# One-step block maxima and first tokens in one stretch, pieces of the second down projection behind five products, late gates kept in SBUF, a denser phase one: a spectral layer with a gated feed-forward on one core

## The chip, the core and the metric

The kernel runs on one core of a Trainium2 chip. The core has a matrix engine (TensorE, PE in the profile; PEld is its weight load), VectorE (DVE), ScalarE (ACT), GpSimd (POOL), and SyncE (SP), whose queue issues all but one of the DMAs. The engines run side by side and wait for each other through semaphores; each takes its own instructions in program order. The metric is the device time in microseconds of one execution. The changed kernel, too, is written for one core.

## What is computed

The input is a sequence of 8192 tokens of width 448. It is normalised; one branch passes it through a Fourier layer (a real FFT over the 8192 positions, a block-diagonal complex two-layer network with four blocks of 112, a soft threshold, the inverse FFT), the other through a gated feed-forward of inner width 1792. The output joins both.

```python
xn = _layernorm(x)                                   # over the 448 channels
Xf = rfft2(xn, axes=(1, 2))                          # 8192 positions
hr = zr @ w1[0] - zi @ w1[1] + b1[0]                 # per block of 112
hi = zi @ w1[0] + zr @ w1[1] + b1[1]
hr, hi = hr * (hr > 0), hi * (hi > 0)
or_ = hr @ w2[0] - hi @ w2[1] + b2[0]
oi_ = hi @ w2[0] + hr @ w2[1] + b2[1]
or_, oi_ = soft(or_, 0.01), soft(oi_, 0.01)          # sign(v) * max(|v| - lam, 0)
s = irfft2(or_ + 1j * oi_)
g = silu((gelu(xn @ w_gate) * (xn @ w_up)) @ w_down)
return x + s * g
```

## The kernel before, in words

**Precision.** All large products run in 16 bit: each operand is split into a high and a low half, scaled by powers of two taken from its largest magnitude, and three of the four partial products are added in PSUM. So a weight tile must first be loaded (`wst`, 704 KB each), its block's maximum found over the whole tile (`gu_block`, `largest`), then be scaled and split (`gu_split`) into its high and low halves in `wt`. `largest` works in two steps: a product with the identity turns the maxima of the 128 partitions into a row (`bf`), VectorE reduces it (`mxr`), and a second product spreads the result over the partitions again. Fourteen weight tiles `f` form eight blocks: tile 0, tile 1, then pairs.

**Tokens.** The 128 x 64 positions are worked in 16 chunks of four tiles of 128 tokens. The feed-forward's inner width goes in two passes: pass 0 takes weight tiles 0 to 7, pass 1 tiles 8 to 13. Chunks 0 and 1 of pass 0 use plain products (`plain`); all others use a 2x2 scheme with seven products instead of eight (`unit`, products 1, 5, 6, 2, 3, 7, 4 in that order, called a1, a5 ... in the code), each `unit` for two weight tiles. For it `gu_comb` prepares sums and differences of the weights (`cb`). Pass 0's down projection goes to DRAM (`prt`); pass 1 adds its own (`down2`, seven products again, in pieces by `prod2`), takes tanh, and writes the gate `q (1 + tanh q)` of every chunk but the last to DRAM (`gsp`).

**The Fourier branch** has three phases: phase one (`chunk1`: normalise, split, first stage, and the transposed tokens to DRAM for the feed-forward), phase two (`group`: second stage, the two layers, threshold) and phase three (`tiles3`: last stage, times the gate from `gsp`, plus `x`, out). They run beside the feed-forward, whose order on PE is fixed by the generator `ffn`.

**What sets the order.** A small planner in the kernel (`Pace`) runs all parts as Python generators on a clock of its own with assumed costs per instruction (`cost`), and emits each engine's instructions in the order in which it meets them; nothing is reordered on the chip. Constants give due times: `T1` and `DT` start phase one's chunks, `END2` and `END3` spread phases two and three, `yield ev(...)` waits in the plan for another part, `pe()` for PE. `Either` (`B`) puts an elementwise operation on VectorE or GpSimd, whichever ends first in the plan.

**Beginning.** `begin` loads the four tiles of chunk 0, computes mean and variance (`stats`: bn_stats, a power on GpSimd, four small steps on VectorE) for tiles 0 and 2, normalises them, then does the same for tiles 1 and 3; `token` splits and transposes each tile on PE into `xta`. Beside it `weights` finds and splits the weight blocks, and starts the maxima of the down weights once tile 1 is split.

**End.** A chunk of pass 1 stops before the last pieces of its `down2`; `state["tail"]` holds them, and the next chunk runs them after two of its first unit's products. The last chunk runs them itself. Each quarter of its gate then waits for phase three's last tiles in `s4`, and is multiplied, added to `x` and stored.

## Time and profile before

| | |
|---|---|
| median of 3 runs | 1820.6 us (1819.4 to 1821.87) |
| profiled execution | 1818.44 us, of which its span 1816.3 us |
| PE busy | 1768.8 us, 97% of the span |
| PE weight loads | 1422.6 us, 78% |
| VectorE busy | 1401.5 us, 77%, 2410 instructions |
| ScalarE busy | 1098.1 us, 60% |
| GpSimd busy | 588.0 us, 32%, 637 instructions |
| DMA | 287.78 MB, mean 158 GB/s; 289 to 328 GB/s in the slices from 1544 to 1771 us |

The profile is one execution. Times in it count from its first instruction; the execution's own time has 2.1 us more than its span. A row of the timeline gives start, duration, engine, source line, operation, tiles, and in brackets how long the engine stood idle before and what released it. All of the kernel's instructions bear one line (that of a recording helper), so they are told apart by their tiles. PE's durations overlap, since products are pipelined: the distance from one start to the next is what a product costs.

### The profile page before, as it was taken

The numbers are of one execution on the slowest core, as the hardware profiler recorded it, in microseconds if no ns is written. First come the engines' busy times: TensorE is split into PE (matmuls) and PEld (weight loads), VectorE is DVE, ScalarE is ACT, GpSimd is POOL, SyncE is SP. The second block draws the span as 40 slices with busy tenths as digits, with TensorE's granted clock in tenths as the row PEclk, the third lists the DMA queues.
The fourth block names the chain that finished last, engine by engine and source line by source line (L and its number), as shares of the span: only waits on it lengthen the run. The fifth ranks groups of instructions, "written<-read, shape, count | busy, mean of one in ns | idle before, by whom it ended". The sixth has DMA issues, their size and how long they took to land. (4 is left out here: it accounts for less than half of the span.)

```text
span 1816.3 us, 39111 instructions
## 1 busy us (share of the span) xinstructions
PE 1768.8 (97%) x15649; PEld 1422.6 (78%) x15649; DVE 1401.5 (77%) x2410; ACT 1098.1 (60%) x2105; POOL 588.0 (32%) x637
## 2 busy tenths in 40 slices
PE   6999999999999999999999999999999999999997
PEld 3446677767777677787887899999998998888886
DVE  7857778867777665666766888888878887878888
ACT  4736566645566555566767777777777765444443
POOL 3324443422443432000101223435343432433332
PEclk9999999999999999999999999999999999999999
DMA  6444665466666454113336634443434436999985
GB/s 254 154 124 152 172 193 157 149 195 185 180 183 194 134 152 126 38 55 100 78 103 174 157 93 119 118 105 87 115 91 118 114 89 171 321 293 328 289 295 184
DMA packets 345654, 287.78 MB, mean 158 GB/s; under 512 B 231840, under 2 KB 312736, under 8 KB 345472
## 3 DMA queue, kind: packets, MB, share of 16 engines
q1 hardware_dynamic: 345328, 285.26, 54.2%
q8 instruction: 122, 2.00, 0.5%
q14 instruction: 60, 0.49, 0.1%
q10 hardware_dynamic: 144, 0.03, 0.0%
HBM read 129.47 MB, written 106.61 MB: 130 GB/s over the span
## 5 line engine op out<-in xcount | busy, mean ns | idle before, releaser
L182 PEld LDWEIGHTS <-wt 128*128 128x128 f16 x9350 | 907.0, 98 | 181.8 <-issue 18.5
L182 PE MATMUL bk<-xta,wt 128*128 128x256 f16 (+1 forms) x5190 | 636.2, 276 | 11.7 <-ACT u L182 4.8
L182 PE MATMUL bk<-xtb,wt 128*128 128x256 f16 x3120 | 382.0, 273 | 1.7 <-ACT v L182 1.7
L182 PE MATMUL bk<-dw,h 128*128 128x448 f16 (+1 forms) x2208 | 373.4, 320 | 4.9 <-DVE h L182 3.3
L182 PEld LDWEIGHTS <-h 128*128 128x128 f16 x2688 | 258.4, 98 | 136.6 <-DVE h L182 4.9
L182 ACT COPY v<-bk 128x512 f32<-128x512 f32 x208 | 121.4, 584 | 89.8 <-PE bk L182 89.1
L182 ACT COPY u<-bk 128x512 f32<-128x512 f32 x208 | 121.5, 585 | 76.7 <-PE bk L182 73.4
L182 POOL TENSOR_TENSOR wt<-wt 128x256 f32<-128x256 f32 x100 | 78.5, 785 | 216.3 <-DVE wt L182 159.8
L182 DVE TENSOR_TENSOR u<-bk,u 128x512 f32<-128x512 f32 x104 | 71.5, 688 | 79.1 <-PE bk L182 73.7
L182 POOL TENSOR_TENSOR zs<-t,zs 112x256 f16<-112x256 f32 (+2 forms) x34 | 30.0, 884 | 262.0 <-ACT zs L182 258.7
L182 PE MATMUL bk<-dw,wt 128*128 128x224 f16 (+1 forms) x864 | 104.0, 269 | 4.8 <-DVE pt L182 4.8
L182 ACT ACTIVATE u<-u,fc 128x512 f32<-128x512 f32 (+1 forms) x118 | 77.7, 669 | 44.5 <-DVE u L182 44.1
L182 DVE SCALAR_TENSOR_TENSOR pt<-bk,fb,pt 128x448 f32<-128x448 f32 x112 | 75.2, 678 | 35.8 <-PE bk L182 35.0
L182 ACT ACTIVATE th<-bk,fb 128x448 f32<-128x448 f32 x64 | 40.4, 633 | 99.2 <-PE bk L182 63.6
L182 ACT CAST h<-wt 128x512 f16<-128x512 f32 (+1 forms) x128 | 68.6, 538 | 41.1 <-DVE wt L182 31.9
L182 DVE TENSOR_TENSOR v<-bk,v 128x512 f32<-128x512 f32 x104 | 71.2, 684 | 19.7 <-PE bk L182 19.1
L182 PE MATMUL bf<-w2t,wn 112*128 112x112 f16 x1512 | 84.9, 213 | 0.0
L182 PEld LDWEIGHTS <-wn 112*128 112x128 f16 x1512 | 80.7, 98 | 3.0
L182 POOL TENSOR_TENSOR v<-v,u 128x512 f32<-128x512 f32 x32 | 47.5, 1485 | 97.1 <-ACT v L182 96.9
L182 PEld LDWEIGHTS <-w1t 112*112 112x112 f16 x612 | 68.1, 130 | 7.6 <-issue 3.4
L182 ACT ACTIVATE th<-pt 128x448 f32<-128x448 f32 x64 | 36.8, 576 | 58.8 <-DVE pt L182 48.9
L182 DVE SCALAR_TENSOR_TENSOR gl<-v,fc,gl 128x512 f32<-128x512 f32 (+1 forms) x70 | 47.1, 690 | 32.4 <-ACT gl L182 31.0
(198 smaller groups left out, 2978.3 us busy)
## 6 DMA issues: line engine op xcount, KB each, us to landing
wst<-in_gu SPq DMA_DIRECT2D x22, 704.0 KB, 5.3
xts<-sx SPq DMA_DIRECT2D x32, 480.0 KB, 3.0
x<-in_x SPq DMA_DIRECT2D x17, 896.0 KB, 6.2
t<-ysb SPq DMA_DIRECT2D x64, 224.0 KB, 3.1
prt<-th SPq DMA_DIRECT2D x64, 224.0 KB, 2.0
pt<-prt SPq DMA_DIRECT2D x64, 224.0 KB, 3.9
u<-t SPq DMA_DIRECT2D x32, 448.0 KB, 5.9
y<-t SPq DMA_DIRECT2D x30, 448.0 KB, 3.5
```

Source lines behind the costliest of these rows:

```text
L182: return self.pace.issue(self.name, kind, out, ins, lambda: fn(out, *args, **kw))
```

## The change

- **Maxima.** For up to four columns `largest` sends each column, broadcast over 128 columns, through a product with the identity, which leaves the 128 partition maxima as a row on every partition, and one reduction on VectorE ends it. The floor moves into the operation before.
- **First tokens.** The statistics of all four tiles come first, on two small tiles of their own; then tiles 0 and 2 are normalised, then block 0's maximum runs with the second root between its product and its reduction, then tiles 1 and 3. The identity's cast moves from VectorE to ScalarE. The planner chooses the engine of the copies into `xta`. The first plain product pair takes high weights ahead of low ones.
- **Weights.** Blocks 1 to 4 are started after tile 0, the down weights' maxima after tile 4 instead of tile 1.
- **Phase one** begins at 78 instead of 84 on the planner's clock and takes 36 instead of 40 per chunk; `END2` and `END3` are 10 and 30 earlier.
- **Pass 1's down projection.** `down2` stops after three products' first pieces; the rest comes in five pieces, behind products a1, a5, a6, a2 and a3 of the next chunk's first unit. The last chunk has an order of its own (`down2_last`): four accumulations, and the two last quarters end behind the same last product.
- **Gates.** Chunks whose gates are not yet made when phase three is opened keep them in SBUF, in `s4`, which chunk 15 used alone before: chunks 9 to 14. Their tiles of phase three run when the chunk's `down2` has begun, and `s4` is handed on by an event (`gfree`).
- **Planner's cost** of a 16-bit copy on VectorE, and more operations of the end left to `Either`.

```diff
-    def largest(dst, src, floor):
+    def largest(dst, src, floor, between=None):
...
+        if w <= 4:
+            for i in range(w):
+                T.matmul(b[:, 128 * i:128 * i + 128], src[:, i:i + 1].to_broadcast([128, 128]), identf,
+                         start=True, stop=True)
...
+            V.tensor_reduce(dst, b[:, 0:128 * w].rearrange("p (i k) -> p i k", i=w), axis=AXIS.X, op=ALU.max)
...
-    T1, DT = 84.0, 40.0
+    T1, DT = 78.0, 36.0
...
-            V.tensor_tensor(mx, fm[:, 0, :, b], fm[:, 1, :, b], op=ALU.max)
+            V.scalar_tensor_tensor(mx, fm[:, 0, :, b], 2.0 ** -30, fm[:, 1, :, b], op0=ALU.max, op1=ALU.max)
...
-        yield from largest(mxa, mx, 2.0 ** -30)
+        yield from largest(mxa, mx, 2.0 ** -30, None if b else (ev("reduced"), ev("root")))
...
     def down2(i, h, last):
+        done("pre", i)
         yield from last()
         x = yield from BD.get()
         yield from prod2(1, i, h, x, 0, 2, first=True)
-        z = yield from BY.get()
+        z = yield from BD.get()
         yield from prod2(2, i, h, z, 0, 2, first=True)
         y = yield from BD.get()
         yield from prod2(5, i, h, y, 0, 2, first=True)
-        yield from prod2(1, i, h, x, 2, 3)
-        e = pace.spawn(add2(i, QS[0], x), pace.last)
-        yield from prod2(2, i, h, z, 2, 3, last=True)
-        yield e
-        pace.spawn(ended2(i, QS[0], z, BY), pace.last)
-        yield from prod2(6, i, h, x, 0, 2)
...
+        def after_a1():
+            yield from prod2(1, i, h, x, 2, 3)
+            m[1] = pace.spawn(add2(i, QS[0], x), pace.last)
+            yield from prod2(2, i, h, z, 2, 3, last=True)
...
+        def after_a5():
+            yield m[1]
+            yield from prod2(6, i, h, x, 0, 2)
...
-        state["tail"] = tail
+        state["tail"] = [after_a1, after_a5, after_a6, after_a2, after_a3]
+
+    def down2_last(i, h, last):
...
     def ended2(i, qq, b, R):
...
+        if state.get("direct", NG) <= i < NG - 1:
+            if state["direct"] < i:
+                yield ev("gfree", i - 1)
+            V.scalar_tensor_tensor(blk(state["last"][0], *qq), th, 1.0, q, op0=ALU.add, op1=ALU.mult)
...
-    END1, END2, END3 = T1 + NG * DT + 12.0, 1460.0, 1780.0
+    END1, END2, END3 = T1 + NG * DT + 12.0, 1450.0, 1750.0
...
     def phase3():
...
+        def near():
+            for i in range(i0, NG):
+                if i < NG - 1:
+                    yield ev("pre", i)
+                for c in (2 * i, 2 * i + 1):
+                    pace.spawn(load3(c))
...
     def weights():
...
-        for b in range(PB[0][1]):
+        pace.spawn(gu_block(0, 0))
+        yield ev("w", 0)
+        for b in range(1, PB[0][1]):
             pace.spawn(gu_block(b, 0))
         combs = pace.spawn(gu_combs(near))
-        yield ev("w", 1)
+        yield ev("w", 4)
```

The order that the planner makes of it is seen at three places. First VectorE at the beginning, around block 0's maximum (`fm`, `fx`, `mxr`; `st` are the statistics, `x_102` is chunk 0's tokens), in the kernel before:

```order
L182 TENSOR_SCALAR x_102<-x_102,st 128x448
L182 TENSOR_REDUCE fm<-wst 128x2
L182 TENSOR_SCALAR x_102<-x_102,st 128x448
L182 COPY fx<-fm 128x2
L182 BN_STATS st<-x_102 128x6
L182 BN_AGGR st<-st 128x2
L182 BN_STATS st<-x_102 128x6
L182 BN_AGGR st<-st 128x2
L182 TENSOR_SCALAR st<-st 128x2
L182 TENSOR_REDUCE mxr<-bf 2x1
L182 TENSOR_TENSOR xs<-x_102,xs 128x448
L182 TENSOR_SCALAR fx<-bf 128x2
```

and in the changed kernel:

```order
L184 TENSOR_SCALAR x_102<-x_102,st 128x448 x2
L184 TENSOR_REDUCE fm<-wst 128x2
L184 TENSOR_SCALAR fx<-fm 128x2
L184 TENSOR_TENSOR st<-st 128x2 x2
L184 TENSOR_SCALAR st<-st 128x2
L184 TENSOR_TENSOR st<-st 128x2
L184 TENSOR_TENSOR xs<-x_102,xs 128x448
L184 TENSOR_REDUCE fx<-bf 128x2
```

Four statistics and one reduction no longer stand between the block's maximum and its factors; both normalisations of tiles 0 and 2 now stand ahead of the weight tile's reduction.

Second VectorE at a change of chunk in pass 1, one of the late ones. `pt` are the four quarters of the chunk that ends, each added to twice out of a PSUM bank; `u1` and `v1` belong to the first unit of the next chunk; `th` and `s4` take the gates. Before:

```order
L182 SCALAR_TENSOR_TENSOR pt_22156<-bk1_67,fb_79,pt_22156 128x448
L182 SCALAR_TENSOR_TENSOR pt_22257<-bk0_66,fb_79,pt_22257 128x448
L182 SCALAR_TENSOR_TENSOR pt_22156<-bk0_66,fb_79,pt_22156 128x448
L182 SCALAR_TENSOR_TENSOR pt_22257<-bk1_67,fb_79,pt_22257 128x448
L182 SCALAR_TENSOR_TENSOR g2_22546<-bf_22679,ms_92,g2_22546 128x448
L182 SCALAR_TENSOR_TENSOR th_22690<-th_22690,pt_22156 128x448
L182 SCALAR_TENSOR_TENSOR pt_22365<-bk0_66,fb_79,pt_22365 128x448
L182 TENSOR_TENSOR u1_22619<-bk3_69,u1_22619 128x512
```

and now:

```order
L184 SCALAR_TENSOR_TENSOR pt_22184<-bk1_67,fb_79,pt_22184 128x448
L184 SCALAR_TENSOR_TENSOR pt_22245<-bk0_66,fb_79,pt_22245 128x448
L184 SCALAR_TENSOR_TENSOR g2_22504<-bf_22673,ms_92,g2_22504 128x448
L184 TENSOR_TENSOR u1_22586<-bk2_68,u1_22586 128x512
L184 TENSOR_TENSOR x2_22502<-g2_22504,x2_22502 128x448
L184 SCALAR_TENSOR_TENSOR pt_22184<-bk0_66,fb_79,pt_22184 128x448
L184 SCALAR_TENSOR_TENSOR g2_22504<-bf_22716,ms_92,g2_22504 128x448
L184 TENSOR_TENSOR v1_22659<-bk4_70,v1_22659 128x512
L184 SCALAR_TENSOR_TENSOR pt_22245<-bk1_67,fb_79,pt_22245 128x448
L184 SCALAR_TENSOR_TENSOR s4_19980<-th_22740,pt_22184 128x2x224
```

The additions of the ending chunk, which stood in one run ahead of the next unit, are now spread among that unit's own additions.

Third VectorE at the very end, before:

```order
L182 SCALAR_TENSOR_TENSOR pt_23403<-bk1_67,fb_79,pt_23403 128x448
L182 TENSOR_TENSOR s4_20190<-pt_23315,s4_20190 128x2x224
L182 SCALAR_TENSOR_TENSOR th_23821<-th_23821,s4_20190 128x448
L182 TENSOR_TENSOR th_23821<-th_23821,x4l_20191 128x448
L182 TENSOR_TENSOR s4_20190<-pt_23403,s4_20190 128x2x224
L182 SCALAR_TENSOR_TENSOR th_23835<-th_23835,s4_20190 128x448
L182 TENSOR_TENSOR th_23835<-th_23835,x4l_20191 128x448
L182 SCALAR_TENSOR_TENSOR pt_23511<-bk0_66,fb_79,pt_23511 128x448
L182 TENSOR_TENSOR s4_20190<-pt_23511,s4_20190 128x2x224
L182 SCALAR_TENSOR_TENSOR th_23852<-th_23852,s4_20190 128x448
L182 TENSOR_TENSOR th_23852<-th_23852,x4l_20191 128x448
```

and now:

```order
L184 SCALAR_TENSOR_TENSOR pt_23341<-bk1_67,fb_79,pt_23341 128x448
L184 SCALAR_TENSOR_TENSOR pt_23414<-bk1_67,fb_79,pt_23414 128x448
L184 SCALAR_TENSOR_TENSOR th_23770<-th_23770,s4_19980 128x448
L184 TENSOR_TENSOR s4_19980<-pt_23341,s4_19980 128x2x224
L184 TENSOR_TENSOR th_23770<-th_23770,x4l_19981 128x448
L184 SCALAR_TENSOR_TENSOR th_23781<-th_23781,s4_19980 128x448
L184 TENSOR_TENSOR th_23781<-th_23781,x4l_19981 128x448
L184 TENSOR_TENSOR s4_19980<-pt_23414,s4_19980 128x2x224
L184 SCALAR_TENSOR_TENSOR th_23790<-th_23790,s4_19980 128x448
L184 TENSOR_TENSOR th_23790<-th_23790,x4l_19981 128x448
```

Two additions out of the last bank, and the rest of three quarters, now stand behind the last product; before it was one quarter's addition, and its three further steps.

228 lines of the change are left out of this document (175 added, 53 removed).

## The prediction

> **What bounds the kernel now.** I read the page first, then a table of windows, the waits by window, and the timeline of the two ends and of one change of chunk.
>
> ```profile
> PE 1768.8 (97%) x15649; PEld 1422.6 (78%) x15649; DVE 1401.5 (77%) x2410; ACT 1098.1 (60%) x2105; POOL 588.0 (32%) x637
> ```
>
> PE is busy 97% of the span, so only its idle time can be won, 47 us in all; the change takes away no product to speak of. The windows (busy time of PE, PEld, DVE, ACT, POOL, then granted clock, DMA share, GB/s) say where that idle time lies:
>
> ```profile
> 0.00:10.00 10.00, 0.75 (x4) 0.37 (x4) 4.14 (x12) 2.05 (x3) 2.04 (x7) 1.00 0.76 267
> 10.00:20.00 10.00, 4.37 (x22) 2.20 (x22) 9.52 (x26) 4.79 (x9) 3.23 (x3) 1.00 0.64 261
> 40.00:50.00 10.00, 8.48 (x51) 4.05 (x49) 10.00 (x20) 4.31 (x10) 4.62 (x5) 1.00 0.73 282
> 50.00:60.00 10.00, 8.28 (x47) 3.90 (x45) 8.97 (x25) 8.25 (x19) 3.59 (x3) 1.00 0.12 25
> 100.00:800.00 700.00, 692.88 (x5246) 508.14 (x5245) 498.06 (x899) 399.02 (x729) 230.98 (x287) 1.00 0.54 153
> 800.00:1500.00 700.00, 695.99 (x7322) 617.04 (x7320) 564.11 (x953) 503.15 (x1025) 209.74 (x198) 1.00 0.42 109
> 1500.00:1800.00 300.00, 292.07 (x2613) 252.30 (x2612) 247.18 (x364) 136.23 (x243) 111.08 (x105) 1.00 0.87 279
> 1800.00:1810.00 10.00, 6.45 (x61) 5.59 (x59) 7.65 (x12) 1.79 (x3) 1.14 (x1) 1.00 0.21 78
> 1810.00:1816.30 6.30, 0.00 (x0) 0.00 (x0) 3.14 (x6) 0.58 (x1) 0.00 (x0) 0.52 0.29 95
> ```
>
> In the first 20 us PE idles 14.9, from 40 to 60 us 3.2, from 100 to 800 us 7.1, from 800 to 1500 us 4.0, from 1500 to 1800 us 7.9, behind 1800 us 9.9. The opening has more idle time than it shows, since a product's duration covers the gaps to the next. The products of the first 57.2 us, by shape:
>
> ```profile
> L182 PE MATMUL bk<-xta,wt 128*128 128x512 f16 x72 | 17.6, 380 | 0.0
> L182 PE MATMUL bk<-xta,wt 128*128 128x256 f16 x44 | 7.6, 316 | 4.9 <-DVE wt L182 3.1 <-ACT wt L182 1.8
> L182 PE MATMUL bf<-xs,m 128*128 128x448 f16 x18 | 4.4, 353 | 0.0
> ```
>
> In a full run of such products (below) one of 256 columns comes every 0.11 us, so one of 512 costs about 0.215 and one of 448 0.19: 72, 44 and 18 of them are 15.5 + 4.8 + 3.4 us, and the 64 transposes, at under 0.11 each, and the maxima add some 6. So PE had about 30 us of work in 57 us. There the kernel is bound by the weights, which VectorE, ScalarE and GpSimd must make ready.
>
> **The opening, worked through the new order.** These rows of the timeline are what the old opening waits for:
>
> ```profile
> 8.95 1.22 DVE L182 TENSOR_REDUCE fm<-wst 128x2 f32<-128x1024 f32 x1 [1.47 <-DMA wst<-in_gu]
> 10.72 0.59 PE L182 MATMUL bf<-identf,fx 128*2 128x128 f32 x2 [1.84 <-DVE fx L182]
> 13.70 0.16 DVE L182 TENSOR_SCALAR fe<-fx 128x2 int32<-128x2 int32 x1
> 14.90 1.32 ACT L182 ACTIVATE wt<-wst,fc 128x512 f16<-128x512 f32 x2
> 17.74 2.25 DVE L182 SCALAR_TENSOR_TENSOR wt<-wst,fc,wt 128x512 f16<-128x512 f32 x2
> 23.47 1.80 PE L182 MATMUL bk<-xta,wt 128*128 128x256 f16 x8
> 23.58 0.62 DVE L182 COPY xta<-bk 128x896 f16<-128x896 f16 x1
> 27.70 1.70 PE L182 MATMUL bk<-xta,wt 128*128 128x256 f16 x14
> 30.55 2.32 PE L182 MATMUL bk<-xta,wt 128*128 128x256 f16 x11
> 31.05 0.66 DVE L182 TENSOR_TENSOR wt<-wst,wt 128x512 f16<-128x512 f32 x1
> 40.26 0.61 DVE L182 TENSOR_REDUCE dmx<-wo 128x1 f32<-128x448 f32 x1
> 41.38 0.98 DVE L182 TENSOR_TENSOR fx<-fm 128x2 f32<-128x2 f32 x1
> 52.64 0.16 DVE L182 TENSOR_SCALAR fe<-fx 128x2 int32<-128x2 int32 x1
> 55.74 1.16 POOL L182 TENSOR_TENSOR wt<-wst,wt 128x512 f16<-128x512 f32 x1 [3.04 <-ACT wt L182]
> 57.21 1.90 PE L182 MATMUL bk<-xta,wt 128*128 128x512 f16 x8
> ```
>
> Weight tile 0 lands at 8.95 whatever the order. Now two normalisations, about half a microsecond each, stand ahead of its reduction: it ends at 11.2 rather than 10.17. The pair of products with the identity is twice as long (the row at 10.72: 0.59 with its tail), to about 12.5; the second root and a split hide behind it, one reduction ends at 13.2, and three small steps at 13.8, where the old one was at 13.86. So block 0 gains nothing; behind it two copies of tokens stand ahead of ScalarE's split, which ends at 16.9 instead of 16.22. What is won stands later on VectorE: nothing is left between, so tile 0's low halves end at 18.4 instead of 19.99. The remaining tokens are in `xta` at 24.6, no sooner than the old 24.2. Block 1's product stands on PE behind the first 22 products and the transposes, to about 23; its factors follow at 24.2, ScalarE's four steps at 27.2, the last low half at 28.5, where the row at 31.05 ends at 31.71. Weight tile 1's products start at 28, where the old ones start at 30.55: **2.5 us** is the lower bound.
>
> The upper bound comes from tile 4. It waited for block 3's maximum, 11 us from `fx` at 41.38 to `fe` at 52.64, because two products and two reductions stood in queues among the down weights' reductions (eight like that at 40.26, 4.9 us on a VectorE that is busy 10.00 of 10). Now that is one product and one reduction, and the eight come after tile 4. From 28 on each tile is 22 x 0.215 plus a first-stage group of 0.57, 5.3 us, so tile 4 can start at 28 + 15.9 = 44 instead of 57.21; my count of the work of ScalarE and VectorE up to there ends at 43.4. What PE had done of chunk 1 by 57.2, 32 transposes and two first-stage groups, 3.5 us, is then still to do. That leaves **9.7 us**; with some waits left I take **8**. Bounds 2.5 and 11.
>
> **A rule on PE's clock.** Eight products take 1.80 us at 23.47 and fourteen 1.70 at 27.70: 0.21 and 0.11 us from start to start, though the windows show 1.00. The Trainium skill (TensorE: Matmul & The Clock Gate, Part 1: The HAM clock gate) says that the array runs at half clock until it has been busy for some 3.4 us, and falls back after as long an idle stretch. The durations agree with it, the granted clock in the table does not show it. By that rule the new opening, with a longer idle stretch ahead of its products, might run all of its first products slow.
>
> **Phase one, denser.** Same work on other due times. It is hidden as far as PE, busy 692.88 of 700, stays fed. The largest waits there:
>
> ```profile
> PE bk L182 <- ACT u L182: 4.8, 2, 3.4
> ```
>
> One of these, of 3.4 us, is a chance of due times; the new ones may lose it or make another. I take 0, bounds -4 and +4.
>
> **Pieces behind five products.** PE's waits from 800 to 1500 us (first row) and from 1500 to 1800 us:
>
> ```profile
> PE bk L182 <- DVE pt L182: 1.8, 6, 0.7
> PE bk L182 <- DVE h L182: 2.9, 5, 1.1
> PE bk L182 <- DVE pt L182: 2.2, 10, 0.3
> PE bk L182 <- ACT h L182: 0.6, 2, 0.3
> ```
>
> `pt` and `h` are those of the down projection: the additions that free a bank for the next piece, and the last unit's halves, needed by the pieces ahead of the next chunk. With six or more products between, 1.3 us each, both are covered. At most 1.8 + 2.9 + 2.2 + 0.6 = 7.5 us; the last chunk's share stays. I take **4.5**, bounds 0 and 7.5.
>
> **Gates in SBUF.** Six chunks drop their stores and loads of
>
> ```profile
> L182 SPq DMA_DIRECT2D gsp<-th x60: 539/551/1614, 1047.6 to 1771.7; - x60
> L182 SPq DMA_DIRECT2D g<-gsp x30: 326/434/1587, 1526.9 to 1785.5; - x30
> mt<-c_mt SPq DMA_DIRECT2D x32, 192.0 KB, 6.5
> ```
>
> 24 of 60 and 12 of 30 (the third row, from the page's list of issues, is a table that every tile of phase three loads: 6.5 us from issue to landing). The last 300 us have the DMA at 0.87, but PE's waits there name a DMA for 0.4 us in all, so this is worth nothing by itself. In return a late chunk's eight additions and products of phase three stand in one stretch of VectorE (busy 247 of 300), and 53 elementwise operations leave GpSimd for it. I take a loss of **1**, bounds -1 and +6.
>
> **The end.**
>
> ```profile
> 1803.67 1.31 PE L182 MATMUL bk<-dw,wt 128*128 128x224 f16 x12 [1.57 <-DVE pt L182]
> 1807.48 0.74 PE L182 MATMUL bk<-wt,h 128*128 128x224 f16 x6
> 1810.62 0.68 DVE L182 SCALAR_TENSOR_TENSOR pt<-bk,fb,pt 128x448 f32<-128x448 f32 x1
> 1812.71 0.63 DVE L182 TENSOR_TENSOR th<-th,x4l 128x448 f32<-128x448 f32 x1
> ```
>
> PE ends at 1808.2 and VectorE 5.1 later. The new order loses the wait of 1.57 and the smaller ones, 2 us at most. But two quarters now hang on the last product: ten VectorE operations of 0.62 to 0.68 stand behind it, 6.4 us instead of 5.1. I take a gain of **0.5**, bounds -1.5 (a loss) and 2.5.
>
> **Sum.** 1818.4 (the execution shown) - 8 - 4.5 + 1 - 0.5 = 1806.4. The median of the runs lies 2.2 above that execution: **1808.6**; I say 1808.
>
> **Rivals.**
> 1. *The weights stay late.* VectorE, at 9 to 10 of 10 between 30 and 60 us, still sets the pace, and only tile 1's 2.5 us arrive. For it: the maximum of block 0 is no sooner. Against it: five microseconds of reductions are gone from that stretch. 1808 + 5.5 = 1813.
> 2. *The pieces bring nothing*: they wait for the same VectorE, which has more to do. For it: `pt` now stands among the unit's additions. 1808 + 4.5 = 1812.
> 3. *Slower: one `s4` for six chunks.* A gate may only be written when the last chunk's tiles of phase three are added. If those come late, by their loads behind a full DMA, the writing instruction stands first on VectorE, and behind it the additions `u1` and `v1` on which PE's next products depend. Against it: a chunk has some 49 us for it (fifteen chunks' stores of `gsp` lie between 1047.6 and 1771.7). It decides from 12 : 6 = 2 us per chunk; with the table's landing of 6.5 us late in five of the six, half of it hidden, 16 us: 1824.
> 4. *All of it arrives*: 11 + 7.5 + 2.5 and no loss: 1820.6 - 21 = 1799.6, or 1797 with a phase one that loses its wait.
> 5. *A slow first stretch.* All of the first tile's 44 products come at 0.21 instead of 0.11: 4.4 us, of which the old opening, with 14 of them, paid 1.4. Up to 3 us of the 8 go: 1811. The Trainium skill (TensorE: Matmul & The Clock Gate, Part 1: The HAM clock gate) has a rule of this kind, told above.
>
> **How the numbers follow.** Forecast 0.50, rivals 0.14, 0.11, 0.08, 0.13, 0.04. Two medians of this kernel can be told apart from about 0.2%, 3.6 us. The forecast's own bounds reach from 1797 to just under 1820.6; the range 1797 to 1819 leaves out the slower rival and the far ends. Faster by over 0.2% means below 1817: all but the slower rival and the upper ends of the others, 0.83; the same 0.10; slower 0.07.
>
> **What would show it.** Right: `fm` near 10 us and one `fx` reduction near 13; weight tile 4's products near 44 to 47 us and PE full from there; no `dmx` reduction before that; PE's waits for `pt` and `h` behind 800 us under 3 us; PE's last product some 6 us ahead of VectorE's last. Wrong: VectorE or ScalarE holding weight tiles 2 to 4 past 50 us; waits of PE for `u` or `v` in the late chunks, behind an `s4` write on VectorE; or new waits between 100 and 800 us of the size of the gain.

## The result and the profile after

The changed kernel takes **1802.2 us** (median of 1799.7, 1802.21 and 1802.29) against 1821.2 us for the kernel before beside it: a ratio of **0.9891, interval 0.9878 to 0.9905**, or 19 us less. Executions that the record marks as slow are left out (6600.5 us of this kernel, 4794.9 us of the one with three `th` below, 2050.1 us of the one before); the second of them is the profiled one, so that kernel has no usable trace. The prediction said 1808, between 1797 and 1819. The total is inside the range. The parts that were to make it up are not what the prediction took them for, as the experiments show.

The page of the changed kernel, first part (busy time, share of the span, instructions):

```profile
span 1800.5 us, 38996 instructions
PE 1763.0 (98%) x15653; PEld 1427.5 (79%) x15653; DVE 1405.0 (78%) x2457; ACT 1100.5 (61%) x2103; POOL 541.4 (30%) x584
```

The work is the same (VectorE 1405.0 us for 1401.5), GpSimd has 47 us less, and the span is 15.8 us shorter. The profiled execution of before (1818.4 us) lies under all its other ones on record, so the traces show 16 of the 19 us. The windows, in the columns of the prediction:

```profile
10.00:20.00 10.00, 6.86 (x36) 4.51 (x37) 7.03 (x18) 4.61 (x10) 3.01 (x3) 1.00 0.74 286
40.00:50.00 10.00, 10.00 (x58) 5.17 (x57) 8.82 (x19) 9.68 (x20) 5.46 (x5) 1.00 0.94 313
50.00:60.00 10.00, 10.00 (x57) 4.93 (x56) 10.00 (x23) 7.58 (x16) 5.35 (x5) 1.00 0.75 256
100.00:800.00 700.00, 692.14 (x5346) 512.31 (x5345) 523.39 (x945) 411.11 (x761) 216.64 (x272) 1.00 0.55 156
800.00:1500.00 700.00, 695.88 (x7252) 617.84 (x7250) 554.30 (x954) 495.87 (x1002) 181.60 (x168) 1.00 0.42 106
1500.00:1785.00 285.00, 284.15 (x2561) 248.55 (x2560) 237.88 (x362) 131.74 (x231) 104.57 (x96) 1.00 0.86 257
```

PE is full from 30 to 60 us. In the two long stretches its idle time has hardly moved (7.9 us for 7.1, 4.1 for 4.0). From 1500 to 1785 us 0.85 us is left; before it was 7.0 in the same window (the prediction's 7.9 reach to 1800).

**Where PE stands.** The number of products is the same but for four, all of them products of the maxima, so the two kernels can be compared at equal work: for each I added up the columns of all products (those of the maxima left out) in order of their starts, and took the time at which the same sum is reached. This is the lead over the kernel before, in us; a minus is a lag. The other rows are the kernels of the experiments below.

| kernel | at 100 us | 500 | 1000 | 1500 | 1700 | 1780 |
|---|---|---|---|---|---|---|
| changed | 6.8 | 3.6 | 4.3 | 5.4 | 12.3 | 15.3 |
| changed, old opening | -0.7 | -2.8 | -2.0 | 2.8 | 4.9 | 7.8 |
| changed, down weights' maxima early | 5.3 | 1.2 | 1.8 | 2.0 | 6.3 | 8.1 |
| changed, old pieces | 6.3 | 4.7 | 5.4 | 0.3 | 3.0 | 3.1 |
| changed, gates through DRAM | 6.6 | 3.7 | 4.4 | 5.4 | 10.3 | 10.3 |
| changed, old phase one | 6.4 | 9.1 | 8.6 | 2.1 | 6.2 | 8.9 |
| before, new opening | 4.7 | 7.4 | 4.7 | 0.7 | -5.0 | -5.5 |
| before, pieces | 0.6 | -1.5 | -1.5 | -5.7 | -3.3 | -1.0 |
| before, dense phase one | -2.0 | -4.7 | -4.0 | -10.8 | -14.5 | -17.8 |
| before, pieces and dense phase one | -0.4 | -2.9 | -2.2 | 2.6 | 0.9 | 2.7 |

Each row is one execution, so small differences are no evidence. The new opening put alone into the kernel before, for one, was profiled in an execution of 1828.1 us, where its median is 1824.1, and the dense phase one alone in one of 1838.9, where it is 1835.0. A microsecond or so at 100 us can come from PE's rate: 6 to 25 of the first weight tile's 44 products came at half rate in these traces (0.21 us from start to start instead of 0.11), and with the same new opening 11 to 18.

The changed kernel wins 6.8 us in the opening, loses 3 of them in phase one by 500 us, wins 1.8 from there to 1500 us and 10 behind that.

**The opening.** Rows of the timeline of the changed kernel, in the order in which the prediction worked through them:

```profile
9.82 1.22 DVE L184 TENSOR_REDUCE fm<-wst 128x2 f32<-128x1024 f32 x1
...
11.39 1.20 PE L184 MATMUL bf<-identf,fx 128*128 128x128 f32 x4 [11.39 <-DVE st L184]
...
13.37 0.16 DVE L184 TENSOR_SCALAR fe<-fx 128x2 int32<-128x2 int32 x1
...
16.92 1.42 DVE L184 SCALAR_TENSOR_TENSOR wt<-wst,fc,wt 128x512 f16<-128x512 f32 x2 [2.55 <-ACT wt L184]
...
16.94 2.53 PE L184 MATMUL bk<-xta,wt 128*128 128x256 f16 x11 [1.75 <-ACT wt L184]
...
23.28 0.91 ACT L184 COPY xta<-bk 128x896 f16<-128x896 f16 x1 [0.42 <-PE bk L184]
...
24.18 0.19 ACT L184 ACTIVATE fc<-fh 128x1 f32<-128x1 f32 x1
...
28.21 0.59 PE L184 MATMUL bk<-xta,wt 128*128 128x512 f16 x2
...
44.93 0.82 PE L184 MATMUL bk<-xta,wt 128*128 128x512 f16 x3
```

Block 0's maximum is done at 13.5 us (worked out: 13.8), tile 0's low halves at 18.34 (18.4), the tokens at 24.2 (24.6), block 1's factors at 24.4 (24.2). Weight tile 1's first product starts at 28.21 (28), weight tile 4's, the 67th of 512 columns, at 44.93 (44). In the kernel before the 67th starts here:

```profile
55.50 0.82 PE L182 MATMUL bk<-xta,wt 128*128 128x512 f16 x3
```

The prediction's row at 57.21 was thus already inside tile 4. The eight reductions of the down weights follow where the prediction has them, four of them being

```profile
L184 DVE TENSOR_REDUCE dmx<-wo x4: 604/605/607, 52.8 to 60.2; 128x1 f32<-128x448 f32 x4
```

(instances; least, median and largest ns; first and last start), all behind 52 us, while PE no longer waits for them.

**The waits of PE**, from 800 to 1500 us (first row) and from 1500 to 1785 us (what is waited for; us in all, times, longest):

```profile
PE bf L184 <- DVE k L184: 4.1, 6, 1.1
PE bf L184 <- DMA mt<-c_mt: 0.5, 1, 0.5
PE bk L184 <- DVE h L184: 0.4, 1, 0.4
```

Not one wait for `pt` is left, and of 2.9 + 0.6 us for `h` 0.4; the 1.7 us for `v` behind 1500 us that the kernel before had, too, are gone. In their place phase two costs more (`k`: 4.1 us for 2.0).

**The end.**

```profile
1790.31 1.28 DVE L184 SCALAR_TENSOR_TENSOR pt<-bk,fb,pt 128x448 f32<-128x448 f32 x2 [1.04 <-PE bk L184]
...
1795.38 0.58 ACT L184 ACTIVATE th<-pt 128x448 f32<-128x448 f32 x1 [3.77 <-DMA out<-th]
...
1796.65 0.62 DVE L184 TENSOR_TENSOR th<-th,x4l 128x448 f32<-128x448 f32 x1
```

VectorE's last operation ends 7.0 us after the last two sums began, as two quarters hang on the last product, and one of the four tanh waits 3.77 us for a store, since there are only two buffers `th`. The lead of 15.3 us at 1780 us is 15.8 at the end: the end is worth half a microsecond.

### The profile page after: what moved, and what is told of

The parts are those of the page before. It is cut to its first block, busy times and chain, and to the rows that moved or that the text cites. A ratio compares the mean times of both kernels' runs of the same rounds, so it can differ in the third digit from the quotient of the medians.

```text
span 1800.5 us, 38996 instructions
## 1 busy us (share of the span) xinstructions
PE 1763.0 (98%) x15653; PEld 1427.5 (79%) x15653; DVE 1405.0 (78%) x2457; ACT 1100.5 (61%) x2103; POOL 541.4 (30%) x584
## 4 chain that ended last, share of the span: by engine, by line
PE 91%; DVE 5%; DMA 2%; issue 1%; ACT 1%; SPq 0%; POOL 0%; ACTq 0%; DVEq 0%
PE bk L184 75%; PE bf L184 16%; DVE wt L184 1%; DMA prt<-th 1%; DMA mt<-c_mt 0%; DVE st L184 0%; DVE h L184 0%; DVE v L184 0%; SPq L184 0%; DVE u L184 0%; DMA x<-in_x 0%; DVE o L184 0%; DVE gl L184 0%; ACT xta L184 0%; DVE cb L184 0%
## 5 line engine op out<-in xcount | busy, mean ns | idle before, releaser
L184 POOL TENSOR_TENSOR wt<-wt 128x256 f32<-128x256 f32 x82 | 70.0, 853 | 254.0 <-DVE wt L184 238.8
L184 POOL TENSOR_TENSOR v<-v,u 128x512 f32<-128x512 f32 x36 | 52.4, 1455 | 83.6 <-ACT v L184 69.6
L184 POOL TENSOR_TENSOR h<-wt,h 128x256 f16<-128x256 f32 (+1 forms) x51 | 54.5, 1069 | 54.2 <-ACT h L184 45.5
L184 DVE SCALAR_TENSOR_TENSOR o<-bf,ms,b2s 128x448 f32<-128x448 f32 (+1 forms) x65 | 43.8, 673 | 32.6 <-PE bf L184 32.5
```

Source lines behind the costliest of these rows:

```text
L184: return self.pace.issue(self.name, kind, out, ins, lambda: fn(out, *args, **kw))
```

## The experiments

Each part was taken out of the changed kernel, and three of them were put alone into the kernel before. Ratios are to the kernel before, with their intervals; its median was 1821.6, 1822.9 and 1821.1 us in the three series (the first row is the result's own, beside 1821.2).

| kernel | us | ratio |
|---|---|---|
| changed | 1802.2 | 0.9891 (0.9878 to 0.9905) |
| changed, old opening | 1809.5 | 0.9933 (0.9917 to 0.9949) |
| changed, old pieces | 1815.9 | 0.9968 (0.9957 to 0.9979) |
| changed, gates through DRAM | 1814.3 | 0.9957 (0.9941 to 0.9973) |
| changed, old phase one | 1828.1 | 1.0032 (1.0020 to 1.0044) |
| changed, down weights' maxima early | 1810.3 | 0.9942 (0.9927 to 0.9957) |
| before, new opening | 1824.1 | 1.0016 (1.0006 to 1.0025) |
| before, pieces | 1848.2 | 1.0143 (1.0119 to 1.0167) |
| before, dense phase one | 1835.0 | 1.0082 (1.0066 to 1.0099) |
| before, pieces and dense phase one | 1818.3 | 0.9990 (0.9981 to 1.0000) |
| before, pieces and gates in SBUF | 1834.5 | 1.0069 (1.0050 to 1.0088) |
| changed, three `th` | 1799.3 | 0.9871 (0.9854 to 0.9889) |
| changed, three `th`, PE busy early | 1800.5 | 0.9889 (0.9874 to 0.9904) |

### The opening, out and alone

Taken out: `largest` in two steps, `begin`, `weights`, the plain products' order and the engine of the first copies, all as before, with the planner's cost of a copy and the start of phase one's first chunk. Alone: the same lines put into the kernel before. Two places of the first; without the lines taken out, `largest` goes its two steps for every width:

```diff
-        if w <= 4:
...
-            V.tensor_reduce(dst, b[:, 0:128 * w].rearrange("p (i k) -> p i k", i=w), axis=AXIS.X, op=ALU.max)
...
-        yield ev("w", 4)
+        yield ev("w", 1)
```

Expected of the first:

> The changed kernel with the opening of the kernel before: two-step maxima, token statistics two tiles at a time, the down weights' maxima behind tile 1; all else as changed. Theory (opening): in the traces PE stands 6.8 us ahead of the kernel before from 60 to 150 us, and this lead is kept to the end, so 1802 + 7 = 1809. Rival (absorbed): phase one loses 3 us behind 150 us, and would lose less without the lead, since its due times then fit; the opening is worth only half of its lead, 1805.

Expected of the second:

> The kernel before with the new opening alone (with the planner's cost of a copy and phase one's first chunk due at 26). Theory (opening): 1821 - 7 = 1814. By the prediction's term of 8: 1813; by its lower bound (only tile 1's 2.5 us): 1818.5. Rival (absorbed): a lead of 7 us at 60 us in the trace, but under 4 left at 800 us, 1817.

Measured: 1809.5, so 7.3 us lost by taking it out, as the first theory has it; and 1824.1 alone, 2.5 us **slower** than the kernel before, which none had. The table of leads tells the two apart. Alone, the opening leads by 4.7 us at 100 and at 1000 us, and then it is given back and more: by 1700 us the kernel lags 5 us. Its waits from 1500 us on:

```profile
PE bk L184 <- DVE pt L184: 6.6, 10, 1.8
PE bk L184 <- DVE h L184: 3.7, 5, 1.9
```

In the kernel before these two are 2.2 and 2.9. So the old pieces' waits are no fixed price: another start of the second pass against phases two and three gives others. Phase three also opens later, as its loads of tables show (`mt`, one load for each of its 32 tiles; the times are the first and the last start):

```profile
L184 SPq DMA_DIRECT2D mt<-c_mt x32: 333/685/1470, 1543.7 to 1808.4; - x32
```

In the kernel before they run from 1523.7 to 1791.1. So the late phase three that the next sections are about may be a part of this loss; the two are not separated. And with the opening taken out of the changed kernel, its 7.5 us at 100 us are down to 2.6 at 1500 us (5.4 - 2.8) and up again to 7.5 at 1780. That the final difference equals that of the opening is therefore no sign that the lead is kept; what the opening itself is worth at the end is not shown by these two runs.

### The pieces, out and alone

```diff
-                if u == 0 and n and state.get("tail"):
-                    yield from state["tail"].pop(0)()
+                if (u, n) == (0, 2) and "tail" in state:
+                    yield from state.pop("tail")()
```

with the old `down2` (and the old end of the last chunk) beside it.

> The changed kernel with the old second down projection: the pieces ahead of the next chunk, the tail in one stretch behind two products; gates stay in SBUF. Theory (pieces): the 10 us by which the lead grows behind 1500 us are the pieces' and go with them: 1802 + 10 = 1812, with waits of PE for pt and h behind 800 us back at 6 to 8 us. By the prediction's term, 4.5: 1807. Rival (gates): most of the late gain belongs to the gates that no longer go through DRAM; then at most 1806.

> The kernel before with the pieces of the second down projection behind five products, and the last chunk's own order; gates go through DRAM as before. Theory (pieces): 1821 - 10 = 1811. By the prediction's terms, 4.5 and 0.5: 1816. Rival (gates): under 5 us gained, over 1816, since the gates' loads and stores still stand in the last 300 us.

Taken out they cost 13.7 us, more than the theory's 10, and three times the prediction's 4.5; the waits for `pt` and `h` come back in part (6.4 us for `pt`, 2.1 for `h` behind 800 us). Alone, the kernel takes 1848.2 us: 26.6 **more** than before. Here both theories fail. The lead table has PE only 1 us behind at 1780 us; everything is lost after that. PE's waits from 1500 us on in that kernel:

```profile
PE bf L182 <- DMA mt<-c_mt: 13.3, 4, 7.2
```

and two windows near its end:

```profile
1700.00:1750.00 50.00, 48.23 (x436) 42.02 (x434) 42.20 (x65) 22.19 (x39) 17.17 (x16) 1.00 0.98 304
1800.00:1820.00 20.00, 11.67 (x52) 5.35 (x50) 11.00 (x18) 0.58 (x1) 0.96 (x1) 0.64 0.99 357
```

The feed-forward is done at 1802 us, and PE waits for the tables of phase three's last tiles behind a DMA that is busy 0.98 and 0.99. The tables' loads show why, in the kernel before, in this one, and in the changed kernel:

```profile
L182 SPq DMA_DIRECT2D mt<-c_mt x32: 333/794/1390, 1523.7 to 1791.1; - x32
```

```profile
L182 SPq DMA_DIRECT2D mt<-c_mt x32: 332/724/2408, 1583.4 to 1828.6; - x32
```

```profile
L184 SPq DMA_DIRECT2D mt<-c_mt x32: 427/689/1188, 1502.4 to 1768.0; - x32
```

Phase three opens 60 us late: phase two had not finished. Its last store, of the second stage's result, moved as much:

```profile
L182 SPq DMA_DIRECT2D t<-u x34: 456/578/602, 775.1 to 1517.3; - x34
```

```profile
L182 SPq DMA_DIRECT2D t<-u x34: 456/538/596, 776.5 to 1578.3; - x34
```

(before, and with the pieces alone). Both begin near 776 us. So the pieces do to the planner's order what nobody had priced: phase two ends late against the feed-forward, phase three opens late, and its 32 tiles, about 2 MB of transfers each (192 KB of tables, 448 KB of `u` by the page's list of issues, and 128 x 896 numbers of 4 bytes, 448 KB, each of `x`, gate and output), must pass in 262 us (1583 to the end at 1845) instead of 293. Why the order comes out so is taken up with the square below.

### Gates through DRAM, old phase one, and a partner for the pieces

```diff
-        i0 = state["direct"] = state["gates"] + 1
-        far = 2 * i0
+        i0, far = NG, 2 * NG
+        state["direct"] = NG - 1
...
-        dt = (END3 - t0 - 40.0) / far
+        dt = (END3 + 30.0 - t0 - 12.0) / far
```

> The changed kernel with every gate but the last chunk's through DRAM, as before; pieces, opening and phase one as changed, phase three over all tiles at an even pace. Theory (a full DMA at the end): with the pieces alone the profile shows phase three opened 59 us late and the DMA at 0.94 to 0.99 from 1600 us on; here it opens as in the changed kernel, near 1500 us, but carries 24 stores and 12 loads more, 10.8 MB, some 36 us of a DMA at 300 GB/s, on a stretch that has about 40 us of it free: most of what is free goes, PE waits for tables and gates in the last 100 us, 1802 + 10 = 1812. By the prediction, where the gates in SBUF are a loss of 1: 1801, by its bounds 1796 to 1803.

```diff
-    T1, DT = 78.0, 36.0
+    T1, DT = 84.0, 40.0
...
-    END1, END2, END3 = T1 + NG * DT + 12.0, 1450.0, 1750.0
+    END1, END2, END3 = T1 + NG * DT + 12.0, 1460.0, 1780.0
```

> The changed kernel with phase one at 84 and 40 and the old end times of phases two and three; all else as changed. Theory (late phase three): phase one ends 57 us later, phase two is squeezed, phase three opens near 1580 instead of 1500 us: some 15 us lost, 1817, with waits for k in phase two and for tables of phase three at the end. By the prediction's term (0, bounds -4 and +4): 1802, 1798 to 1806.

The kernel before with the new `down2`, `ended2` and phase three's new order together:

> The kernel before with the pieces and the gates in SBUF together, old opening, old phase one with its end times. Tells which partner the pieces need. Theory (late phase three): phase two is stretched by the pieces as in the run with them alone and phase three opens near 1580 us; the gates in SBUF take load from the DMA but the tiles have to pass in the remaining 230 us: 1825. Rival (gates suffice): without the jam behind 1780 us the pieces bring their 13: 1808.

Measured 1814.3, 1828.1 and 1834.5: gates in SBUF are worth 12.1 us, the dense phase one 25.9, in the company of the rest, and gates in SBUF do not rescue the pieces without it. The edit of phase one holds both its own due times and the end times of phases two and three; which of them opens phase three earlier was not tried apart. The theory of a late phase three holds in direction each time: the first and the last load of tables are

```profile
L184 SPq DMA_DIRECT2D mt<-c_mt x32: 440/678/1356, 1575.6 to 1805.5; - x32
```

```profile
L182 SPq DMA_DIRECT2D mt<-c_mt x32: 454/676/1062, 1585.1 to 1814.0; - x32
```

with the old phase one, and with pieces and gates. In the first PE waits 9.3 us for tables from 1500 us on, where the changed kernel waits 0.5. The losses are 11 and 9 us larger than the theory said.

Of the gates: up to 1600 us the two kernels agree (8.5 and 8.4 us of lead), then the one with gates through DRAM stops gaining. DMA share and GB/s (last two columns) from 1500 to 1780 us, with gates through DRAM and in the changed kernel:

```profile
1500.00:1780.00 280.00, 275.15 (x2481) 240.94 (x2479) 227.86 (x340) 126.21 (x222) 111.72 (x100) 1.00 0.96 296
```

```profile
1500.00:1780.00 280.00, 279.15 (x2509) 243.55 (x2508) 233.12 (x355) 129.95 (x228) 103.24 (x95) 1.00 0.87 262
```

PE idles 4.0 us more in the first. Its waits there name ScalarE, no DMA. The second row is ScalarE's own, in the same 280 us:

```profile
PE bk L184 <- ACT v L184: 4.8, 4, 2.2
```

```profile
ACT th L184 <- DMA gsp<-th: 9.1, 4, 3.3
```

So ScalarE stands 9.1 us for stores of gates, with two buffers `th`, and VectorE 13.3 us for ScalarE's `th` behind it; in the changed kernel ScalarE has no such wait there. Two of the stalls end at 1629.0 and 1717.9 us, 4 and 17 us ahead of PE's waits at 1633.1 and 1734.9; that they make them is not shown. The other 7 us are lost behind 1780 us, where its last tiles of phase three come at 1797.6 and 1798.7 us. The pace of phase three in this kernel is mine (32 tiles evenly to the old end), so part of the 12.1 us may be the pace and not the gates.

### The square: pieces and dense phase one

```diff
-    T1, DT = 84.0, 40.0
+    T1, DT = 78.0, 36.0
...
-    END1, END2, END3 = T1 + NG * DT + 12.0, 1460.0, 1780.0
+    END1, END2, END3 = T1 + NG * DT + 12.0, 1450.0, 1750.0
```

in the kernel before, alone and with the pieces.

> The kernel before with the denser phase one and its end times alone (78, 36, 10 and 30 sooner). Theory (late phase three): phase three opens some 30 to 50 us sooner than at 1524 us, but with the old pieces PE's waits for pt and h stay and no jam was there to be taken away: 1820, between 1817 and 1824. Rival (a gain by itself): earlier loads of phase three thin out the full DMA, and its waits behind 1500 us go from 8 to 3 us: 1815. By the prediction's term: 0, -4 to +4.

> The kernel before with the pieces behind five products and the denser phase one; gates through DRAM, old opening. Together with the run of the pieces alone and of phase one alone this closes a square. Theory (late phase three): phase three opens near 1500 instead of 1583 us and the jam at the end of the pieces alone goes, 1848 - 27 = 1821; measured from the other side, the changed kernel without gates in SBUF (1814) and without the opening's 7: 1821. Rival (gates through DRAM jam whatever the start): 1835 or more.

Measured 1835.0 and 1818.3. With the kernel before and the pieces alone this is a square of ratios: neither 1, pieces 1.0143, phase one 1.0082, both 0.9990. If the two did not touch each other, both would give 1.0226; they give 2.4% less, some 43 us (the pieces alone are of another series than the other two; each ratio is to its own). The theory of the late phase three is right of the pair (1821 expected) and says nothing of the corner that none foresaw, the dense phase one alone at 14 us slower. There phase three opens early, its tables' loads running

```profile
L182 SPq DMA_DIRECT2D mt<-c_mt x32: 333/695/1402, 1487.3 to 1781.6; - x32
```

and PE waits from 1500 to 1800 us, beside 1.9 us for `pt`, for

```profile
PE bk L182 <- ACT v L182: 4.5, 7, 1.2
PE bk L182 <- DVE h L182: 4.3, 5, 1.2
```

and lags 10.8 us at 1500 us already. Here the feed-forward comes last: the last chunk's first pieces of the down projection stand at

```profile
1811.15 2.46 PE L182 MATMUL bk<-dw,h 128*128 128x224 f16 x24
```

29 us after the last load of tables. Which of the two, early phase three or late feed-forward, makes those waits longer was not tested. The last product of the feed-forward and that of phase three end at these times:

| kernel | feed-forward | phase three |
|---|---|---|
| before | 1808 | 1801 |
| before, pieces | 1802 | 1834 |
| before, dense phase one | 1829 | 1802 |
| before, pieces and dense phase one | 1805 | 1786 |
| changed | 1790 | 1779 |

So either of the two alone ends one branch about 30 us behind the other, with phase three late or the feed-forward late, and neither is late with both. That is what the runs show. That the distance between the branches is itself the cause is not shown: with both it is still 20 us, and with the dense phase one alone PE idles 5 us more than before already from 1000 to 1500 us (8.7 for 3.6). Why phase two falls back by 60 us under the pieces with the old phase one, and by none with the dense one (its last store is at 1481.8 us with phase one alone and at 1483.4 with both), is a matter of the planner's order that I have not settled.

The runs also hold one way from the kernel before to the changed one on which each step is a gain: pieces and dense phase one together 1818.3, gates in SBUF added 1809.5 (the changed kernel with the old opening), the new opening added 1802.2.

### The down weights' maxima early

```diff
-        yield ev("w", 4)
+        yield ev("w", 1)
         yield pace.spawn(down_weights(0))
```

> The changed kernel with the down weights' maxima started behind tile 1 again instead of tile 4; one-step maxima and the new order of the first tokens stay. Theory of the prediction (the eight reductions, 4.9 us of VectorE between 40 and 55 us, held tile 4): weight tile 4's products begin 4 to 5 us later than at 44.9 us, PE's lead at 100 us falls from 6.8 to 2.5, and the time is 1802 + 4 = 1806. Rival (the one-step maximum is what counts, since a block's product and reduction no longer queue twice): the lead falls by under 1.5 us, 1803.

Weight tile 4 begins at

```profile
46.13 1.04 PE L184 MATMUL bk<-xta,wt 128*128 128x512 f16 x4
```

instead of 44.93, and the lead at 100 us is 5.3 instead of 6.8. But tile 1 is as late in this execution, and its first reduction of a down weight starts only at 37.0 us:

```profile
29.42 0.59 PE L184 MATMUL bk<-xta,wt 128*128 128x512 f16 x2
```

That is 1.2 us behind 28.21, as 18 of tile 0's 44 products come at half rate here and 14 in the changed kernel's trace. From tile 1 to tile 4 it is 16.7 us in both. So the rival is right of the opening, and more than right: the reductions of the down weights cost tile 4 nothing that these traces show, and what brought it 10 us forward lies in the rest, the one-step maximum and the order around it, which were not tried apart. The time is another matter: 1810.3, 8 us more, by which both theories fail. Behind 1500 us PE waits 3.5 us for `v` again. The order of products on PE differs from the changed kernel's from 39 us on, so one line of the beginning gives the planner another order for the whole run; at which place that costs 8 us was not followed.

### Three buffers, and an array that is busy early

```diff
-    TH = ring(fp, [128, D], F32, "th", 2)
+    TH = ring(fp, [128, D], F32, "th", 3)
```

> The changed kernel with three buffers th instead of two. In its profile ScalarE stands 8.0 us before a tanh's or a copy's write to th until the store of the buffer is out (at 324.9 us), and PE waits 2.9 us behind that at 329.9 us; at the end the last tanh waits 3.8 us for a store of the output, and VectorE 1.07 us for it. Theory: the end comes 1.1 us sooner and PE's 2.9 us go: 1798 to 1801. Rival: the stall near 325 us is the store's own lateness, which holds up others too, and only the end's 1.1 us come: 1801.

```diff
+        for i in range(80):
+            nc.tensor.matmul(BD.free[-1][:, 0:128], ident, ident, start=True, stop=True)
```

> The changed kernel with three buffers th, and with 80 products of the identity with itself into an unused bank ahead of the first product (their results are overwritten; everything else is the same order). In the profile of the changed kernel PE is idle to 11.39 us, the 13 products of tile 0 from 16.94 us come at 0.213 us and only from about 20.4 us at 0.109; VectorE stands 1.57 us for block 1's product at 22.94 us. Theory (the first stretch runs at half rate because PE was idle, rival 5 of the prediction): busy from 3.3 us, the transposes end a microsecond sooner, the 13 products cost 1.4 instead of 2.8 us, block 1's maximum and with it all weight tiles come 2 us sooner; PE's lead at 100 us grows by 2, and with the buffer's 2 to 3 us the time is 1797. Rival (VectorE sets the pace): the products come at 0.109 from the start but the lead at 100 us grows by less than 0.5: 1799.

Measured 1799.3 and 1800.5. Both have the third buffer, and their intervals overlap with the changed kernel's, so neither is shown to be faster than it; by the ratios the gain, if it is one, is 0.4 to 3.6 us. The trace of the second shows what the buffer does:

```profile
1789.66 1.28 DVE L184 SCALAR_TENSOR_TENSOR pt<-bk,fb,pt 128x448 f32<-128x448 f32 x2 [1.04 <-PE bk L184]
...
1794.06 1.15 DVE L184 TENSOR_TENSOR th<-th,x4l 128x448 f32<-128x448 f32 x2
...
327.44 1.12 ACT L184 ACTIVATE wo<-wst,fc 128x256 f16<-128x256 f32 x2 [7.65 <-DMA prt<-th]
...
329.85 1.61 PE L184 MATMUL bk<-xta,wt 128*128 128x256 f16 x12 [3.72 <-ACT u L184]
```

From the last two sums to VectorE's last operation it is 5.6 us instead of 7.0: the end's 1.4 us are there. The stall near 325 us is not: ScalarE goes on at 327.44 as before, and PE waits until 329.85. The rival is right, and the trace of the changed kernel shows the likely holder, in its view of the tile `wo` from 318 to 330 us:

```profile
L184 SPq DMA_DIRECT2D wsp<-wo x1: 519/519/519, 319.0 to 319.0; - x1
DMA to landing us min/median/max: 8.4/8.4/8.4
```

The only buffer `wo` is stored from 319.0 us on and free 8.4 us later, at 327.4; the splitting that writes it next starts at 327.44, and ScalarE's later work waits behind it. The profile names another store. A second `wo` was not tried.

As for PE's rate, rows of the timeline with PE busy early (the row at 3.28 us is the 80 products):

```profile
3.28 6.29 PE L2026 MATMUL bk<-ident 128*128 128x128 f16 x80 [3.28 <-DMA ident<-c_small]
...
12.46 0.68 PE L184 MATMUL bf<-identf,fx 128*128 128x128 f32 x4 [2.89 <-DVE st L184]
...
12.98 0.50 PE L184 MATMUL bf<-ident,xs 128*128 128x128 f16 x4
...
17.13 2.53 PE L184 MATMUL bk<-xta,wt 128*128 128x256 f16 x11 [1.75 <-ACT wt L184]
```

Of the 80 products the first start 0.107 us apart, and from 6.8 us on 0.056. The maximum's four products take 0.68 us instead of 1.20 and the first four transposes 0.50 instead of 0.77, but from 14 us on they take 0.75 again, and the first products with weights come 0.213 apart to 20.3 us, as in the changed kernel. The lead did not grow: weight tile 1 starts at 28.3 us (28.21). In this execution the tokens landed 1.1 us later; the reduction of block 0's maximum starts 0.8 us later than in the changed kernel, and the first product with weights 0.2. So a gain of up to a microsecond may hide behind the late landing. Whether a busy array to 17 us would bring anything was not tried.

The Trainium skill (TensorE: Matmul & The Clock Gate, Part 1: The HAM clock gate) has the half rate end after some 3.4 us of activity and return after an idle window of about that length. The traces agree in the main: the 80 products were at half rate for 3.5 us from the first, the fall back came 4.4 us behind the last of them, with 1.2 us of work between, and the new opening left the half rate 3.5 us after its products with weights began. But the 3.7 us of maxima and transposes ahead of these, from 11.39 to 15.1 us, had not ended it.

## Why the prediction was right, and where not

The total, 1808 forecast and 1802 measured, is right within its range. Of its five terms the opening and the end are right in size at their own places, the pieces are right in mechanism and too small, and phase one and the gates failed.

**The opening, 8.** The worked chain holds to within a microsecond at each of its steps, tile 1 (28 worked out, 28.21 measured) and tile 4 (44, 44.93) included, and 6.8 us of lead at 100 us is the 8 with "some waits left". (The old tile 1 starts at 30.76; the row at 30.55 still holds two products of tile 0.) Its upper bound rests on a row that is not tile 4's first: with 55.50 for 57.21 the same working gives 8.0 instead of 9.7, and for the 11 that it then takes it names no source. Half of the reason given for that bound is not borne out: that two products and two reductions stood "in queues among the down weights' reductions". With those reductions back in place tile 4 follows tile 1 by the same 16.7 us as in the changed kernel; the two steps of the maximum were not tried apart. And the step from this lead to the end of the program was never taken: the prediction added it as if a lead were kept. It is 3.6 us at 500 us, and alone the opening ends in a loss.

**Phase one, 0.** This is the step that failed furthest: "It is hidden as far as PE ... stays fed". In the stretch itself the bound of 4 is passed: the lead falls by 3.2 us between 100 and 500 us, and with the old phase one it rises by 2.7, a difference of 5.9. By 1500 us this is won back (5.4 for 2.1). What decides comes later: with the edit phase three opens at 1502 us instead of 1576, and 25.9 us are lost without it. The prediction priced the step where it stands and not at the end of the chain that starts with it.

**Pieces behind five products, 4.5.** The waits that were named are gone, 7.5 us but for 0.4, so this is the upper bound, and the mechanism is right where the rest of the change is present. Mis-sized is the bound itself, which has the terms that PE's waits name and none for the order: "At most 1.8 + 2.9 + 2.2 + 0.6". Taken out of the changed kernel they cost 13.7, and alone 26.6 the other way. The prediction kept apart the waits that the pieces remove and the order that the planner makes with them.

**Gates in SBUF, a loss of 1.** Wrong in sign: 12.1 us are lost without them, the pace of phase three included. The step that failed is "PE's waits there name a DMA for 0.4 us in all, so this is worth nothing by itself". With gates through DRAM the DMA is at 0.96 and PE waits for ScalarE, still without naming a DMA; it is ScalarE that waits for the gates' stores, and the last tiles come late. The fear beside it, rival 3, did not come: behind 1500 us PE waits for neither `u` nor `v` in the changed kernel.

**The end, 0.5.** Lead at 1780 us and at the end differ by 0.5, less than one execution differs from another. The ten operations behind the last product are there; what the prediction missed is that a tanh among them waits for a store.

**The rivals.** Rival 1 and 2 fell with the opening and the pieces. Rival 4, all of it arriving, comes nearest in its sum (1799.6), without its reasons. Rival 5 did not cost its 3 us: the new opening has 14 of its products with weights at half rate (11 from 16.94 us and the 3 from 19.96), as many as the prediction counted in the old one, and leaves the half rate at 20.4 us. In other traces with the new opening there are 11 to 18, so a part of it comes in some executions. Rival 4's 1797 is 1796 by its own terms (1799.6 less the wait of 3.4).

Undone one by one, the four larger parts lose 7.3, 13.7, 12.1 and 25.9 us, 59 in all, for a gain of 19. The prediction added them as if each brought its own. Its sum of 12 (8 + 4.5 - 1 + 0.5) came near the 19 by terms of which two are off by 26 and 13, because each was priced beside an unchanged rest: that the total came out is luck as far as these two go, and no proof of the parts. The range, too, is narrower than the terms allow: their bounds, added up, reach from 1795 to 1830, where the prediction says 1797 to just under 1820.6.

## What to carry to other kernels

Where a planner writes the order of two branches that share a full engine, price a change at the place where the branches meet again: ask when the later branch now starts its last phase, and whether its transfers still fit before the end. Parts of such a change are not to be added: a square of four runs (neither, each alone, both) shows whether they may be, and here two parts that each make the kernel slower, by 27 and 14 us, together make it no slower. A wait that names an engine does not clear the DMA: look at what that engine itself waits for, as ScalarE's 9.1 us for the stores of gates show.

## What the runs showed that was not expected

- A late phase three ends in waits for the DMA: opened 60 us later (1583.4 for 1523.7 us), it left PE in waits of up to 7.2 us for one 192 KB table, at a DMA share of 0.95 to 0.99 and 357 GB/s from 1800 to 1830 us.
- One line that starts the down weights' maxima three weight tiles earlier moves the end by 8 us, though from tile 1 to tile 4 no time is lost by it.
- PE's half rate at the beginning lasts differently from trace to trace: with the same new opening 11, 14 or 18 of the first 44 products come at 0.21 us instead of 0.11, which moves weight tile 1 by about a microsecond.
- VectorE's operations with two operands in SBUF take much longer at times. The form below has a least, median and largest duration of 737, 746 and 1767 ns in the changed kernel:

```profile
L184 DVE SCALAR_TENSOR_TENSOR wt<-v,fc,u x48: 737/746/1767, 1024.1 to 1777.2; 128x512 f32<-128x512 f32 x48
```

The pair of tile 0's low halves took 2.25 us before, with a GpSimd operation running beside its first half (16.75 to 18.77 us), and 1.42 in the changed kernel, with GpSimd starting only at 18.02. That GpSimd is the cause was not tested.
